# Ten extra products after the transposes of q for tile 1, in the opening of a fused attention, MLP and soft-MoE kernel

## The chip, the cores and the metric

The kernel runs on one core of a Trainium2 chip. The metric is device microseconds of one execution; a kernel's figure is the median of its runs. The engines are named as in the profile: PE is TensorE (PEld its weight loads), DVE is VectorE, ACT is ScalarE, POOL is GpSimd, and SP issues the DMAs. [...]

## The reference

Three stages follow one another, all in float32.

```
k_p, v_p = means of k and v over 8 neighbouring positions      # 576 -> 72 positions
attn = softmax(q @ k_p.T / 8);  x = attn @ v_p                 # 8 batches, 8 heads, head size 64
x = x.transpose(0, 2, 1, 3).reshape(4608, 512)
x = relu(x @ w_in)**2 @ w_out                                  # 512 -> 2048 -> 512
logits = x @ phi                                               # 32 slots
slots = softmax(logits over tokens).T @ x                      # 32 x 512
slots = relu(slots @ w1[e]) @ w2[e]                            # 8 experts, 4 slots each
out = softmax(logits over slots) @ slots
```

## The kernel before

The 4608 tokens are cut into 36 tiles of 128. A tile goes through attention first, then through the first layer of the MLP (`l1_half`), four quarters of 512 columns each. In the trace the first layer is L453: xh is the rounded high part of the attention's output x of a tile, xl the rest, and each quarter takes twelve products (four chunks of 128 rows; each is xh with the high part of w, xh with the low part of w, and xl with the high part of w).

The steps of attention of a tile t, with their lines:

- `att_qT`: four transposes of q on PE (L218), then one ACT copy into `acc` (L222). Every tile uses the same `acc`.
- `att_sc`: the scores, two halves of two products (L234) on PE; each half has its maxima taken on DVE (L241, `mx`).
- exponentials: tiles 0, 1 and 3 take eight small ACT instructions (L245, `es`); tile 2 adds the maxima on DVE (L250) and takes one ACT instruction (L259).
- `att_norm`: row sums, reciprocal and scaling on DVE (L266, L267, L268; L264 for tile 2).
- `att_aT`: eight transposes on PE (L299), two ACT copies (L300).
- `att_av`: sixteen products on PE (L311), then xh on ACT (L318) and xl on DVE (L319).

Before the first layer can run, w_in has to be converted, a chunk of 128 rows at a time: one ACT instruction (L342), four DVE instructions and one that may run on either (L344, L347, L351, L355, L356; all on DVE here), an ACT cast to the high part (L395) and a POOL subtraction for the low part (L396). The names w_243, w_485 and w_578 in the rows of the order are the first three quarters of w_in before the change (w_243, w_496 and w_589 behind it); l_... are the PSUM tiles of the first layer. es_121 is the buffer of tiles 0 and 2, es_122 that of tiles 1 and 3.

The function `opening` issues tiles 0 to 3 and the first two quarters of w_in by hand; from there slots of a table take over. `early` and `behind` set priorities and order, but the final order on each engine's queue is made by a scheduler when the program is built: each engine runs its own queue strictly in that order, and an instruction that waits holds all that stand behind it on its engine. The opening already holds two groups of products of the identity with itself, whose result nobody reads (named `warm`): eleven before the first data arrive (L957) and six behind the transposes of q of tile 0 (L684, the line of `behind`).

Of the kernel before, what the change touches and what calls it, by code (L numbers as in the profile page):

```python
# [8 lines left out]
F32 = mybir.dt.float32  # L9
# [8 lines left out]
def kernel(  # L18
# [12 lines left out]
    nc = tc.nc  # L31
# [4 lines left out]
    E, _, F = w1.shape  # L36
# [3 lines left out]
    P = 128  # L40
# [28 lines left out]
    ps1 = ctx.enter_context(tc.tile_pool(name="ps1", bufs=1, space=bass.MemoryType.PSUM))  # L69
# [7 lines left out]
    ident = const.tile([P, P], F32, tag="ident", name="ident")  # L77
# [136 lines left out]
    def att_qT(t):  # L214
        qt = q_t.pop(t)
        pq = ps("gT" if t in (0, 2, 4, 6, 8, 10, 12, 14, 16, 18, 20, 22, 24, 26, 28, 29, 30, 31, 33) else "att")
        for i in range(NPAIR):
            mark["q0"] = nc.tensor.transpose(  # L218
                pq[:, i * P:(i + 1) * P], qt[:, 2 * i:2 * i + 2].rearrange("p h d -> p (h d)"), ident
            )  # L220
        qT = acc.rearrange("p (a b) -> p a b", b=P)
        mark["qT", t] = nc.scalar.activation(out=qT.rearrange("p a b -> p (a b)"), in_=pq, func=AF.Copy)  # L222
        qT_t[t] = qT

    def att_sc(t):
        qT = qT_t.pop(t)
        es = es2[t % 2][:, :H * SP].rearrange("p (h s) -> p h s", s=SP)
        mx = a1.tile([P, H], F32, tag="mx", name="mx", bufs=8)
        for half in range(2):
            sc = ps("gT" if t in (0, 2, 4, 6, 8, 10, 12, 14, 16, 18, 20, 22, 24, 26, 28, 29, 30, 31, 33) else "att")  # L230
            for i in range(2):
                pi = 2 * half + i
                for off, n, b, s in parts(t):
                    mark["sc", t] = nc.tensor.matmul(  # L234
                        sc[off:off + n, i * 2 * SP:(i + 1) * 2 * SP],
                        qT[:, pi, off:off + n],
                        kb[b % 2][:, pi].rearrange("p a s -> p (a s)"),
                    )
            sv = sc[:, :HH * SP].rearrange("p (h s) -> p h s", s=SP)
            hs = slice(half * HH, (half + 1) * HH)  # L240
            mark["mx", t] = nc.vector.reduce_max(out=mx[:, hs], in_=sv, axis=AX.X, negate=True)  # L241
            if t in NXS:
                for h in range(HH):
                    e = half * HH + h
                    mark["es", t] = nc.scalar.activation(  # L245
                        out=es[:, e], in_=sv[:, h], func=AF.Exp, bias=mx[:, e:e + 1],
                        accum_out=rsum[:, t % 8, e, 0:1],
                    )
                continue
            nc.vector.tensor_tensor(  # L250
                out=es[:, hs], in0=sv, in1=mx[:, hs].unsqueeze(2).to_broadcast([P, HH, SP]), op=ALU.add
            )
        es_t[t] = es

    def att_exp(t):
        if t in NXS:
            return
        es = es_t[t]
        nc.scalar.activation(out=es, in_=es, func=AF.Exp)  # L259

    def att_norm(t):
        es = es_t[t]
        if t not in NXS:
            nc.vector.reduce_sum(out=rsum[:, t % 8, :, 0], in_=es, axis=AX.X)  # L264
        rs = a1.tile([P, H], F32, tag="rs", name="rs", bufs=4)
        nc.vector.reduce_sum(out=rs, in_=rsum[:, t % 8], axis=AX.X)  # L266
        nc.vector.reciprocal(out=rs, in_=rs)  # L267
        mark["norm", t] = nc.vector.tensor_tensor(out=es, in0=es, in1=rs.unsqueeze(2).to_broadcast([P, H, SP]), op=ALU.mult)  # L268
# [36 lines left out]
    def att_av(t):  # L305
        aT = aT_t.pop(t)
        px = ps("gT" if t in (0, 2, 4, 6, 8, 10, 12, 14, 16, 18, 20, 22, 24, 26, 28, 29, 30, 31, 33) else "att")
        for i in range(NPAIR):
            for off, n, b, s in parts(t):
                for e in range(2):  # L310
                    nc.tensor.matmul(  # L311
                        px[e * D:(e + 1) * D, i * P + off:i * P + off + n],
                        vp_t[b][:, 2 * i + e],
                        aT[:, 2 * i + e, off:off + n],
                    )
        xh = xp.tile([P, KD, P], F32R, tag="xh", name="xh")
        xl = xp.tile([P, KD, P], F32R, tag="xl", name="xl")
        nc.scalar.copy(out=xh.rearrange("p a b -> p (a b)"), in_=px)  # L318
        nc.vector.tensor_tensor(  # L319
            out=xl.rearrange("p a b -> p (a b)"),  # L320
            in0=px,
            in1=xh.rearrange("p a b -> p (a b)").bitcast(F32),
            op=ALU.subtract,
        )
        x_t[t] = (xh, xl)
# [36 lines left out]
    st_t, mark, n_st = {}, {}, [0]  # L362
# [24 lines left out]
    def conv_steps(j, kk):  # L387
        if kk == 0:
            wq.append(wp.tile([P, 2, KD, QF], F32R, tag="w", name=f"w{j}"))
        w = wq[j]  # L390
        steps = f32_steps(st_t["in", j][:, kk], eng=eng[AE[4 * j + kk]])
        for _ in range(3):
            c = next(steps)
            yield
        nc.scalar.copy(out=w[:, 0, kk], in_=c)  # L395
        nc.gpsimd.tensor_tensor(out=w[:, 1, kk], in0=c, in1=w[:, 0, kk].bitcast(F32), op=ALU.subtract)  # L396
        yield
# [282 lines left out]
    def behind(names, fn, *a):  # L680
        with ExitStack() as es:
            for n in names:
                es.enter_context(tc.issue_after(mark[n].ins))
            fn(*a)  # L684
# [5 lines left out]
    def new_big(shape, name, dtype=F32):  # L690
        pool, tag = ring[n_big[0] % len(ring)]
        n_big[0] += 1
        if pool == 1:
            return None, [late[1].tile([P] + shape[2:], dtype, tag=tag, name=name) for _ in range(4)]
        t = (late[pool] if pool in (0, 2) else pool).tile(shape, dtype, tag=tag, name=name)
        return t, [t[:, i] for i in range(4)]
# [73 lines left out]
    def early(fn, *a):  # L770
        with tc.high_priority():
            fn(*a)
# [175 lines left out]
    def opening():  # L948
        conv = {(j, kk): conv_steps(j, kk) for j in range(PC) for kk in range(KD)}

        def go(j, kk, n=4):
            for _ in range(n):
                next(conv[j, kk])

        warm = ps1.tile([P, P], F32, tag="pl", name="warm")
        for _ in range(11):
            nc.tensor.matmul(warm, ident, ident)  # L957
        early(kb_from, 0, pk0)
        go(0, 0, 2)
        early(att_qT, 0)  # L960
        warm = ps1.tile([P, P], F32, tag="pl", name="warm")
        for _ in range(6):
            behind(["q0"], nc.tensor.matmul, warm, ident, ident)
        go(0, 0, 1)
        behind([("qT", 0), "kbA"], go, 0, 0, 1)
        early(att_sc, 0)
        go(0, 1, 1)
        behind(["kbV"], go, 0, 1, 2)
        behind([("es", 0)], go, 0, 1, 1)
        early(att_norm, 0)  # L970
        for i in range(0, NPAIR, 2):
            behind([("sc", 0), ("es", 0)], pool_v, 0, i, kvp)
            behind([("mx", 0) if i == 0 else ("norm", 0)], pool_v_dve, 0, i + 1, kvp)
        go(0, 2, 1)
        behind([("mx", 0)], go, 0, 2, 2)
        behind([("es", 0)], go, 0, 2, 1)
        early(att_aT, 0)
        early(att_av, 0)
        go(0, 3, 3)
        behind([("aT", 0)], go, 0, 3, 1)  # L980
        for half in range(2):
            l1_half(0, 0, half)
        behind(["pv"], att_qT, 1)
        behind([("aT", 0)], att_sc, 1)
        att_norm(1)
        behind([("l1", 0, 0)], att_aT, 1)
        att_av(1)
        for t in (2, 3):
            att_qT(t)
            for kk in range(2):  # L990
                if t == 3:
                    go(1, kk)
            att_sc(t)
            att_exp(t)
            att_norm(t)
            att_aT(t)
            for kk in range(2, 4):
                if t == 3:
                    go(1, kk)
            att_av(t)  # L1000

    opening()
    nc.sync.dma_start(out=phi_sb, in_=phi.rearrange("(k p) s -> p k s", p=P))
    at(5, load_q, 4)
# [77 lines left out]
    cT_rest, _ = new_big([P, NT // 4 - NG, 4, P], "cT", F32R)  # L1082
# [94 lines left out]
```

## Time and profile before

| what | us |
|---|---|
| median of three runs | 774.43 (772.29 to 775.55) |
| the profiled execution | 766.02 |
| its span | 764.2 |

The profiled execution is the one whose trace is read here; its span leaves 1.82 us of its time outside. It is 8.41 us under the median of the runs. In the span PE is busy 95% of the time, DVE 70%, ACT 51%, POOL 17%. The page's line of granted clocks has a 6 for one slice of 40, the second one (19.1 to 38.2 us); in all others but the last it shows 9.

A timeline row reads: start, duration, engine, line, operation, tile written and tile read, shape, count, and in brackets the idle time before and what ended it. The records of a float32 product come in twos. Neighbouring records overlap by some tens of ns, so the step from one start to the next is the better measure of what an instruction costs in a full queue.

### The profile page before, as it was taken

What the parts mean: (1) busy time and instruction counts of PE and PEld (TensorE: products, weight loads), DVE (VectorE), ACT (ScalarE), POOL (GpSimd) and SP (SyncE); (2) the same over time, 40 slices, a digit from 0 to 9 for tenths busy, and PEclk for the clock granted to TensorE, in tenths of its full rate; (3) what the DMA queues carried; (4) which work ended last, traced back from release to release, by engine and by line L of the source; (5) the groups of instructions that cost most, each with busy time, mean ns of one, the idle gap of its engine ahead of it and who ended that gap; (6) DMA issues with size and microseconds to landing.
All of it is one profiled execution on the core that took longest, in us unless ns stands there. A gap on an engine that the chain in (4) does not pass through costs nothing.

```text
span 764.2 us, 14453 instructions
## 1 busy us (share of the span) xinstructions
PE 723.5 (95%) x5260; PEld 511.4 (67%) x5260; DVE 532.0 (70%) x1049; ACT 392.1 (51%) x1135; POOL 132.1 (17%) x151
## 2 busy tenths in 40 slices
PE   8789999989899999999999999999999999998992
PEld 7557788777677776676666666766666676663462
DVE  4996766596936689789979787878787746324153
ACT  3685677455547464545656562737575454341142
POOL 2231300052714400050342221320000000000000
PEclk9699999999999999999999999999999999999997
DMA  8956754858655996696997788878686436979998
GB/s 276 310 181 204 232 134 135 247 146 250 166 166 151 281 250 183 185 275 177 256 285 224 194 243 241 227 216 240 177 271 199 116 96 233 415 250 352 372 313 294
DMA packets 224135, 175.10 MB, mean 229 GB/s; under 512 B 75072, under 2 KB 186688, under 8 KB 224064
## 3 DMA queue, kind: packets, MB, share of 16 engines
q1 hardware_dynamic: 224064, 174.17, 75.2%
q8 instruction: 42, 0.69, 0.4%
q14 instruction: 29, 0.24, 0.1%
HBM read 126.94 MB, written 47.19 MB: 228 GB/s over the span
## 4 chain that ended last, share of the span: by engine, by line
PE 71%; DVE 12%; DMA 7%; ACT 6%; issue 2%; SPq 0%; POOL 0%; ACTq 0%; DVEq 0%
PE l L453 44%; PE misc L633 3%; PE pl L541 3%; PE misc L1098 2%; PE gT L311 2%; ACT es L245 2%; PE att L311 2%; PE l L1066 2%; PE gT L234 2%; PE att L234 2%; PE att L541 2%; DMA kv<-in_v_dram 1%; ACT aT L284 1%; DMA st<-in_moe_w_in_dram 1%; DMA out_dram<-o 1%
## 5 line engine op out<-in xcount | busy, mean ns | idle before, releaser
L453 PE MATMUL l<-w,xh 128*128 128x512 f32 x1152 | 383.4, 412 | 10.1 <-DVE g L473 5.0
L453 PEld LDWEIGHTS l<-w,xh 128*128 128x128 f32 x1152 | 209.8, 190 | 77.1 <-issue 17.1
L453 PE MATMUL l<-w,xl 128*128 128x512 f32 x576 | 231.7, 403 | 0.0
L466 ACT ACTIVATE r<-l 128x512 f32<-128x512 f32 x144 | 86.6, 604 | 163.6 <-PE l L453 151.1
L453 PEld LDWEIGHTS l<-w,xl 128*128 128x128 f32 x576 | 109.3, 190 | 28.7 <-issue 3.9
L157 POOL TENSOR_TENSOR kv<-kv 72x512 f32<-72x512 f32 x40 | 54.0, 1356 | 211.6 <-DMA kv<-in_v_dram 112.8
L284 ACT COPY aT<-turned 32x256 f32<-32x256 f32 (+1 forms) x168 | 67.8, 404 | 21.2 <-DVE turned L293 19.2
L473 DVE TENSOR_TENSOR g<-l,r 128x512 f32<-128x512 f32 x57 | 39.0, 683 | 28.0 <-ACT r L466 21.8
L245 ACT ACTIVATE es<-att,mx 128x72 f32<-128x72 f32 x120 | 36.9, 334 | 25.3 <-DVE mx L241 25.0
L516 DVE STREAM_TRANSPOSE turned<-turned 128x1024 f32<-128x1024 f32 x39 | 47.6, 1230 | 2.5 <-DMA turned<-g_dram 1.9
L245 ACT ACTIVATE es<-gT,mx 128x72 f32<-128x72 f32 x120 | 36.8, 331 | 16.0 <-DVE mx L241 15.9
L286 DVE COPY aT<-turned 32x256 f32<-32x256 f32 (+1 forms) x120 | 38.4, 320 | 1.6
L475 ACT ACTIVATE g<-r 128x512 f32<-128x512 f32 x54 | 34.5, 640 | 0.8
L396 POOL TENSOR_TENSOR w<-tmp,w 128x512 fp32r<-128x512 f32 x16 | 22.8, 1430 | 66.6 <-ACT w L395 66.6
L158 POOL TENSOR_TENSOR kv<-kv 72x256 f32<-72x256 f32 x40 | 33.1, 833 | 0.8
L473 DVE TENSOR_TENSOR tmp<-l,r 128x512 f32<-128x512 f32 x33 | 22.5, 682 | 15.4 <-ACT r L466 12.1
L268 DVE TENSOR_TENSOR es<-es,rs 128x576 f32<-128x576 f32 x36 | 32.3, 902 | 0.7
L344 DVE TENSOR_SCALAR tmp<-tmp 128x512 uint32<-128x512 uint32 x32 | 16.3, 511 | 23.3 <-ACT tmp L342 23.3
L516 DVE STREAM_TRANSPOSE tmp<-tmp 128x1024 f32<-128x1024 f32 x25 | 30.3, 1223 | 2.9 <-DMA tmp<-g_dram 2.9
L342 ACT ACTIVATE tmp<-st 128x512 f32<-128x512 f32 x32 | 21.7, 680 | 14.5 <-DMA st<-in_moe_w_in_dram 10.3
L245 ACT ACTIVATION_READ_ACCUMULATOR es<-att,mx 128x1 f32 x120 | 26.3, 219 | 0.0
L245 ACT ACTIVATION_READ_ACCUMULATOR es<-gT,mx 128x1 f32 x120 | 26.0, 217 | 0.0
(200 smaller groups left out, 1064.1 us busy)
## 6 DMA issues: line engine op xcount, KB each, us to landing
g_dram<-g SPq DMA_DIRECT2D x95, 256.0 KB
turned<-g_dram SPq DMA_DIRECT2D x39, 512.0 KB
w<-in_moe_w_dram SPq DMA_DIRECT2D x32, 512.0 KB
tmp<-g_dram SPq DMA_DIRECT2D x25, 512.0 KB
w<-in_moe_w_dram SPq DMA_DIRECT2D x6, 2048.0 KB
g_back<-g_dram SPq DMA_DIRECT2D x40, 256.0 KB
kv<-in_k_dram SPq DMA_DIRECT2D x32, 288.0 KB
kv<-in_v_dram SPq DMA_DIRECT2D x32, 288.0 KB
```

What stands on the lines that cost most here:

```text
L157: eng.tensor_tensor(out=x[:, :, 0:4], in0=x[:, :, 0:4], in1=x[:, :, 4:8], op=ALU.add)
L158: eng.tensor_tensor(out=x[:, :, 0:2], in0=x[:, :, 0:2], in1=x[:, :, 2:4], op=ALU.add)
L245: mark["es", t] = nc.scalar.activation(out=es[:, e], in_=sv[:, h], func=AF.Exp, bias=mx[:, e:e + 1], accum_out=rsum[:, t % 8, e, 0:1],)
L268: mark["norm", t] = nc.vector.tensor_tensor(out=es, in0=es, in1=rs.unsqueeze(2).to_broadcast([P, H, SP]), op=ALU.mult)
L284: nc.scalar.copy(out=dst, in_=src)
L286: eng[e].tensor_copy(dst, src)
L453: mm = mark["l1", t, j] = nc.tensor.matmul(hp_t[t, j], steps[i][0], steps[i][1], start=(i == 0), stop=(i == 2 * n - 1))
L466: nc.scalar.activation(out=r, in_=hp, func=AF.Relu, scale=1.0 / (R * R if sq == "V" else R))
L473: mark["sq"] = nc.vector.tensor_tensor(out=dst, in0=pre, in1=src, op=ALU.mult)
L475: nc.scalar.activation(out=dst, in_=src, func=AF.Square)
L516: nc.vector.transpose(out=gc.rearrange("p (n i) -> p n i", i=32), in_=gc.rearrange("p (n f) -> p n f", f=32))
L541: mark["logits"] = nc.tensor.matmul(pl[32 * c:32 * c + 32], a_sb[:, c, 32 * j:32 * j + 32], gT[:, c], start=(alone or j == 0), stop=(alone ...
```

## The change

Behind the four transposes of q of tile 1, and ahead of that tile's scores, ten products of the identity with itself are issued into a fresh PSUM tile of the tag `pl`. Nothing reads their result.

```diff
         behind(["pv"], att_qT, 1)
+        warm = ps1.tile([P, P], F32, tag="pl", name="warm")
+        for _ in range(10):
+            mark["warm"] = behind(["q0"], nc.tensor.matmul, warm, ident, ident)
         behind([("aT", 0)], att_sc, 1)
```

The queue of PE at that place, around the transposes of tile 1 (L218) and its scores (L234 into att); rows with + are new:

```order
 L182 MATMUL l_306<-kv_148,ident 72x128 x8
 L218 MATMUL att<-ident,qt 128x128 x4
+L684 MATMUL warm<-ident 128x128 x10
 L234 MATMUL att<-kb_119,acc 128x144 x4
 L299 MATMUL gT<-ident,es_121 72x128 x8
```

The ten products stand between the two steps of tile 1; all that stood ahead of them is as it was. Behind them the scheduler laid out the rest of the opening anew. The queues of PE, ACT and DVE differ from there to the attention of tiles 2 and 3, and from then on all queues hold the same work in the same order; POOL's and SP's do so throughout.

On ACT, the stretch around xh of tile 1 (L318), the copy of q of tile 3 (L222) and the casts of the second quarter of w_in (L395), before:

```order
L342 ACTIVATE tmp<-st 128x512
L259 ACTIVATE es_121<-es_121 128x576
L318 CAST xh<-att 128x512
L222 ACTIVATE acc<-att 128x512
L395 CAST w_485<-tmp 128x512 x2
L245 ACTIVATE es_122,rsum<-att,mx 128x72 x8
```

and now:

```order
L259 ACTIVATE es_121<-es_121 128x576
L300 COPY aT<-att 72x512 x2
L342 ACTIVATE tmp<-st 128x512
L395 CAST w_496<-tmp 128x512
L318 CAST xh<-att 128x512
L222 ACTIVATE acc<-att 128x512
L395 CAST w_496<-tmp 128x512
L245 ACTIVATE es_122,rsum<-att,mx 128x72 x8
```

The third cast of that quarter has moved from behind xh and the copy of q to ahead of them; it waits for a DVE instruction (L356).

On DVE, from the conversion of the second chunk of that quarter (the first L356 here) on, before:

```order
L356 SCALAR_TENSOR_TENSOR tmp<-tmp 128x512
L250 TENSOR_TENSOR es_121<-gT,mx 128x288
L351 SCALAR_TENSOR_TENSOR tmp<-st,tmp 128x512
L241 TENSOR_REDUCE mx<-gT 128x4
L344 TENSOR_SCALAR tmp<-tmp 128x512
L347 TENSOR_SCALAR tmp<-tmp 128x512
L355 TENSOR_TENSOR tmp<-tmp 128x512
L250 TENSOR_TENSOR es_121<-gT,mx 128x288
L351 SCALAR_TENSOR_TENSOR tmp<-st,tmp 128x512
L356 SCALAR_TENSOR_TENSOR tmp<-tmp 128x512
```

and now:

```order
L356 SCALAR_TENSOR_TENSOR tmp<-tmp 128x512
L268 TENSOR_TENSOR es_122<-es_122,rs 128x576
L250 TENSOR_TENSOR es_121<-gT,mx 128x288
L351 SCALAR_TENSOR_TENSOR tmp<-st,tmp 128x512
L344 TENSOR_SCALAR tmp<-tmp 128x512
L347 TENSOR_SCALAR tmp<-tmp 128x512
L355 TENSOR_TENSOR tmp<-tmp 128x512
L264 TENSOR_REDUCE rsum<-es_121 128x8
L351 SCALAR_TENSOR_TENSOR tmp<-st,tmp 128x512
L356 SCALAR_TENSOR_TENSOR tmp<-tmp 128x512
```

The scaling of tile 1 (L268 on es_122) has moved behind the first L356 (it stood four places ahead of it), the row sums of tile 2 (L264) have moved ahead of the second L356, and one half of tile 2's maxima and of L250 have moved ahead of this stretch.

## Rows read from the trace of the kernel before

**Rows 1.** Busy time by stretch; per engine us (count), then PEclk, DMA share, GB/s.

```profile
26.00:30.00 4.00, 4.00 (x27) 3.12 (x26) 4.00 (x8) 3.00 (x12) 0.90 (x1) 0.50 0.91 227
...
40.00:50.00 10.00, 8.22 (x48) 5.49 (x45) 10.00 (x19) 6.57 (x24) 2.98 (x3) 1.00 0.73 246
...
60.00:70.00 10.00, 10.00 (x64) 7.67 (x63) 8.33 (x11) 5.50 (x10) 1.74 (x1) 1.00 0.46 137
```

**Rows 2.** Timeline, opening, three engines: start, duration, engine, line.

```profile
2.04 4.63 PE L957 MATMUL warm<-ident 128*128 128x128 f32 x22 [2.04 <-POOL ident masks.py:199]
...
12.82 1.60 PE L684 MATMUL warm<-ident 128*128 128x128 f32 x12
...
19.73 0.66 PE L218 MATMUL att<-ident,qt 128*128 128x128 f32 x4 [0.47 <-DMA qt<-in_q_dram]
...
22.19 0.62 ACT L222 ACTIVATE acc<-att 128x512 f32<-128x512 f32 x1
...
22.86 2.06 PE L234 MATMUL att<-kb,acc 128*128 128x144 f32 x8 [2.48 <-ACT acc L222]
...
27.34 0.80 DVE L241 TENSOR_REDUCE mx<-att 128x4 f32<-128x288 f32 x2
```

**Rows 3.** Busy time in short stretches around changes of the granted clock.

```profile
23.10:23.20 0.10, 0.10 (x2) 0.10 (x2) 0.10 (x1) 0.00 (x0) 0.10 (x1) 0.68 1.22 440
...
36.70:36.80 0.10, 0.10 (x2) 0.10 (x1) 0.10 (x1) 0.00 (x0) 0.10 (x1) 0.56 1.07 369
...
156.20:156.40 0.20, 0.20 (x3) 0.14 (x2) 0.20 (x2) 0.00 (x0) 0.20 (x1) 0.64 1.11 384
...
159.60:159.80 0.20, 0.20 (x2) 0.12 (x2) 0.20 (x1) 0.20 (x3) 0.20 (x2) 0.83 0.97 346
```

**Rows 4.** Timeline of PE ahead of the second fall of the clock.

```profile
155.01 0.74 PE L453 MATMUL l<-w,xh 128*128 128x512 f32 x2 [1.60 <-DVE g L473]
```

**Rows 5.** Timeline, DVE alone, a stretch with nothing between its instructions.

```profile
41.40 0.44 DVE L250 TENSOR_TENSOR es<-gT,mx 128x288 f32<-128x288 f32 x1
41.76 0.68 DVE L351 SCALAR_TENSOR_TENSOR tmp<-st,tmp 128x512 f32<-128x512 uint32 x1
42.36 0.68 DVE L356 SCALAR_TENSOR_TENSOR tmp<-tmp 128x512 uint32<-128x512 uint32 x1
42.96 0.41 DVE L344 TENSOR_SCALAR tmp<-tmp 128x512 uint32<-128x512 uint32 x1
43.30 0.68 DVE L355 TENSOR_TENSOR tmp<-tmp 128x512 f32<-128x512 f32 x1
43.90 0.74 DVE L264 TENSOR_REDUCE rsum<-es 128x8 f32<-128x576 f32 x1
44.56 1.11 DVE L347 TENSOR_SCALAR tmp<-tmp 128x512 uint32<-128x512 uint32 x1
```

**Rows 6.** Timeline: one POOL run, and a DVE instruction beside the next.

```profile
44.12 1.27 POOL L396 TENSOR_TENSOR w<-tmp,w 128x512 fp32r<-128x512 f32 x1 [3.87 <-ACT w L395]
...
48.31 1.30 DVE L355 TENSOR_TENSOR tmp<-tmp 128x512 f32<-128x512 f32 x1
```

**Rows 7.** Timeline, from xh of tile 1 to the last attention of the opening.

```profile
42.46 0.58 ACT L318 CAST xh<-att 128x512 fp32r<-128x512 f32 x1
...
47.84 0.45 DVE L241 TENSOR_REDUCE mx<-att 128x4 f32<-128x288 f32 x1
...
49.72 0.24 ACT L245 ACTIVATION_READ_ACCUMULATOR es<-att,mx 128x1 f32 x1
...
50.80 0.15 DVE L266 TENSOR_REDUCE rs<-rsum 128x8 f32<-128x16 f32 x1
...
51.23 0.76 DVE L268 TENSOR_TENSOR es<-es,rs 128x576 f32<-128x576 f32 x1
...
52.13 1.04 PE L299 MATMUL att<-ident,es 128*72 128x128 f32 x8 [0.74 <-DVE es L268]
...
55.64 1.14 PE L311 MATMUL att<-aT,vp 72*64 72x128 f32 x16 [0.58 <-ACT aT L300]
```

## The prediction

> **What bounds the kernel now.** I read the page first, then busy time by stretch, then the timeline of the opening. After the opening TensorE is the bound: from 60 to 70 us it is busy for 10.00 of 10 us [rows 1], and this goes on with few gaps to the end. So the change can act in two ways only: it moves the moment at which that dense stretch begins, or it adds work to it. It adds none there; the ten products stand in the opening.
>
> In the opening TensorE is not the bound. From 40 to 50 us VectorE is busy for 10.00 of 10 us and TensorE for 8.22; from 26 to 30 us VectorE again has no gap while TensorE runs at a granted clock of 0.50, and is busy for all of that time only because it takes twice as long [rows 1]. The rows of VectorE there follow each other without a hole: each start is the one before plus 0.34 to 0.66 us [rows 5]. These are the conversions of w_in, the maxima, and the scaling of attention.
>
> The idle time that the change fills is plain: the transposes of q of tile 1 start at 19.73 and end at 20.39, and the scores of that tile start at 22.86, after 2.48 us in which TensorE waited for the copy on ScalarE, which ends at 22.81 [rows 2]. [...] A second fall, at 156.3 until 159.7, came 1.3 us after a gap of 1.60 us [rows 3, 4].
>
> The point where VectorE hands over to TensorE is the end of tile 3's attention. The last maxima of that tile start at 47.84, the last exponential ends at 49.96, two small instructions follow on VectorE from 50.80, the scaling starts at 51.23, the transposes at 52.13, and the last attention products, behind which TensorE never waits for long, at 55.64 [rows 7]. I therefore ask how far the changed order moves that 55.64.
>
> **The ten products.** Six such products took 1.60 us at full clock, 0.267 each; ten take 2.67 us [rows 2]. Begun at 20.39 they end at 23.06, and the scores start 0.2 us late. Were the clock at half, the eleven products at the start of the program give 0.42 each (4.63 over 11) [rows 2]; the ten would then end at 24.6 and the scores start 1.7 us late. Either is covered: the two maxima that read these scores stand on VectorE behind a reduction, a conversion step and more, at 27.34 before [rows 2] and later now; at half clock the scores take 2.06 us [rows 2] and are done at 26.7. Cost 0; without that cover 0.2 to 1.7 us.
>
> **The clock.** With the gap filled I expect the granted clock to stay at 1.00 past 23.2. At most this gives back half of 13.6 us, 6.8 us of TensorE time. I put its worth on the path at 0, since VectorE, with no hole in those stretches [rows 1, 5], does not get its own work done sooner when TensorE is faster.
>
> **What the new order moves.** This is the larger part. Steps from one start to the next are taken from [rows 5]: 0.60 for L351, L355 and L356, 0.34 for L344 (and L347, which has the same shape), 0.36 for L250 (and L241, which is as long), 0.66 for L264 (and L268, over the same 576 columns).
>
> First, ScalarE now has the cast of the third chunk of the second quarter ahead of xh of tile 1 and the copy of q of tile 3. It waits for the second L356 of the rows of the order. Compared with before, only the row sums L264 are newly ahead of that L356 (L268 stands ahead of it in both orders), so it ends at 42.96 + 0.66 = 43.6. The cast takes about as long as the cast L318, 0.58 [rows 7], and xh starts at 44.2 instead of 42.46 [rows 7], 1.7 us later. Behind xh wait the copy of q and then the scores of tile 3. Their maxima are taken far later on VectorE (next step), which covers this. It costs TensorE something else: it has nothing to do between the transposes of tile 3's q, which before ended just ahead of 42.46 where xh starts, and the cast's end at 44.2, a gap of some 1.8 us.
>
> Second, the last maxima of tile 3. Ahead of them stand three instructions that came right behind them before: a reciprocal (a tenth), a conversion step (0.60) and the scaling of tile 2 (0.66), 1.4 us. A third POOL run also falls ahead of them. Beside POOL's subtractions instructions of VectorE are stretched: L347 at 44.56 took 1.11 us where L344, of the same shape, took 0.41, and L355 at 48.31 took 1.30 where it took 0.68 at 43.30 [rows 5, 6]; so one run costs about 0.65. Together 2.0 us: the last maxima end at 48.2 + 2.0 = 50.2. The exponentials end 1.76 us behind them (49.96 less 48.20) [rows 7], at 52.0, and the scaling starts 0.43 later (51.23 less 50.80), at 52.4 instead of 51.23: 1.2 us late. In the old order the scaling stood behind other work of VectorE when the exponentials were done; now VectorE waits for them.
>
> How POOL's runs fall is the unknown. Of each of the three runs VectorE may lose nothing (if what it does there is a reduction or reads PSUM) or the whole 1.27 us of a run [rows 6]. With nothing lost the scaling starts at about 50.3, 0.9 us early; with all lost at about 54.1, 2.9 us late. I take 0.65 a run, as the rows have it.
>
> [...] The stretched rows [rows 5, 6] show a block of about half a run. [...]
>
> Third, the tail. From the scaling to the last attention products it took 55.64 less 51.23, 4.41 us [rows 7]; there ScalarE was late, with squares, copies and xh of tile 2 ahead of the copies of tile 3. In the new order that work is mostly done while VectorE waits. TensorE then does: the start of the transposes 0.90 behind the scaling (52.13 less 51.23), the transposes 1.04 [rows 7], half of tile 2's attention products 0.57 (half of 1.14) [rows 7], the four transposes of tile 4's q 0.66 [rows 2]. That is 3.17 us, 1.24 less.
>
> The sum so far: +1.2 - 1.24 = 0.0, with bounds of -0.9 - 1.24 = -2.1 and +2.9 - 1.24 = +1.7.
>
> Fourth, the gap of 1.8 us on TensorE ahead of the cast is as long as the 1.60 us that was followed by the second fall. If the clock falls there and is back after 3.4 us as in that case [rows 3, 4], TensorE does 1.7 us less work. In 40 to 50 us it had 1.78 us without work [rows 1], so most of it is covered; between 0 and 1.7 us I take 0.4.
>
> So the profiled execution of 766.02 us becomes 766.4. Against the median of the runs, which lies 8.41 us higher, the same +0.4 gives **774.8 us**: no change that can be told. A difference under 0.5% (3.9 us) is about what a measurement of this kernel can't tell from none.
>
> **The rivals.**
>
> *The dummies don't hold the clock.* At full clock the scores take half of 2.06 us and are done at 24.1; then TensorE waits for VectorE to scale tile 0. If the clock falls a few us later than before, it is at half until about the same 36.8 [rows 3]. The order is the new one all the same. The half of the scores that VectorE wants first then costs it at most the 1.03 us by which they take longer; I take 0.6. For it: work that takes half the time leaves gaps about as long as before. Against it: the one long gap, 2.48 us, is filled. Time: 774.8 + 0.6 = 775.4.
>
> [...]
>
> *The clock falls late (slower).* The gap ahead of the cast, about 42.4 to 44.2, is followed by a fall as long as the first, 13.6 us, just where the products of the second quarter and tile 3 stand. Half of that, 6.8 us, is lost, less the 1.78 us of idle time of 40 to 50 us [rows 1]: +5.0 over the sum of 0.0, or 779.4 us. It decides when the gap grows beyond 1.6 us and the clock isn't back by 50 us. For it: the gap is new, and the first fall lasted that long [rows 3]. Against it: the second fall, amid dense products, lasted 3.4 us only.
>
> *TensorE is the bound after all (faster).* Then the 6.8 us at half clock come back, less 0.2 for the products: 774.43 - 6.6 = 767.8. For it: 13.6 us at half clock in a kernel that TensorE bounds. Against it: VectorE has no hole from 26 to 30 and from 40 to 50 us [rows 1].
>
> **How the numbers follow.** Forecast 0.53; the clock not held 0.17; the whole lock 0.08; the late fall 0.13; TensorE the bound 0.09. The first three lie within 0.5% of 774.43 (770.6 to 778.3), 0.78; a part of 0.01 on each side for what the later waits make of a shift, which leaves same 0.76, faster 0.10, slower 0.14. The forecast's own range is 772.3 to 776.5 (-2.1 to +2.1 around the median, the upper end 1.7 and 0.4). For 8 in 10 it reaches toward the faster and the slower case: 770.0 to 779.0.
>
> **What would show it.** Right: granted clock 1.00 from 23 to 27 us; ten products from 20.4 to about 23.1; no hole on VectorE until the last maxima of tile 3, then a wait of about 1 us for the exponentials; xh of tile 1 at about 44.2, a TensorE gap of about 1.8 us before it; the last attention products within 2 us of 55.6. Wrong: VectorE idle between 23 and 45 us, so that TensorE sets the pace there; those last products before 53 or after 58 us; or a shift made in the opening that is gone or doubled by 200 us.

## The result, and the profile after

The changed kernel is slower: a median of 778.95 us over 6 runs (778.17 to 780.06) against 772.69 over 6 runs of the kernel before beside it (769.76 to 775.55). The ratio is 1.008, with a 95% interval of 1.0053 to 1.0108: 0.8%, some 6 us. The median lies 0.05 us inside the upper end of the predicted range, which was drawn that wide for the slower rival; that is luck. The forecast, no change that can be told, is wrong. Here and below a ratio is that of the runs within 1.5% of the fastest of their kernel, and not the quotient of the two medians, which are of all runs. The profiled execution took 779.36 us, its span is 777.6.

Busy time by stretch of the kernel after, the same columns as in [rows 1]:

```profile
10.50:20.50 10.00, 10.00 (x118) 9.86 (x115) 4.73 (x10) 3.45 (x6) 1.29 (x1) 0.50 1.02 293
24.80:27.00 2.20, 2.20 (x22) 2.20 (x21) 2.20 (x5) 1.27 (x3) 1.33 (x1) 1.00 1.01 275
27.00:28.20 1.20, 1.16 (x10) 0.94 (x8) 1.20 (x4) 0.69 (x1) 0.01 (x1) 1.00 0.87 153
34.70:40.90 6.20, 5.46 (x14) 4.07 (x15) 5.62 (x11) 4.27 (x20) 1.82 (x1) 0.50 0.99 330
45.00:55.00 10.00, 7.96 (x46) 5.92 (x45) 10.00 (x17) 4.46 (x8) 4.31 (x3) 0.83 0.51 165
51.80:54.60 2.80, 2.80 (x12) 2.40 (x10) 2.80 (x4) 0.62 (x1) 1.52 (x2) 0.50 0.99 379
65.00:71.50 6.50, 6.50 (x42) 5.25 (x38) 2.54 (x4) 1.25 (x3) 1.26 (x1) 0.50 0.17 46
72.00:80.00 8.00, 8.00 (x56) 6.05 (x55) 5.63 (x11) 4.98 (x9) 1.39 (x1) 1.00 0.42 115
```

From 45 to 55 us VectorE is busy for 10.00 of 10 us, as from 40 to 50 before; from 27.0 to 28.2 the scores run at full clock; and the half-speed stretch (granted clock 0.50) that came at 23.2 and lasted until 36.8 before, 13.6 us [rows 3], now comes at 34.2 and lasts 6.8. The first row is not the change's doing. The clock stood at 0.50 from about 10 to 20 us, ahead of all that was changed, and it did so in 9 of the 14 profiles of this study, the kernel before among them. It puts the transposes of q of tile 1 at 24.34 instead of 19.73; in the nine profiles they start at 22.77 to 25.98, in the other five at 19.73 to 20.55. From here on I therefore count from the start of those transposes, and call it S.

TensorE in the changed kernel (start, duration, line), to be laid beside [rows 2, 7]:

```profile
24.34 0.60 PE L218 MATMUL att<-ident,qt 128*128 128x128 f32 x4
24.78 2.40 PE L684 MATMUL warm<-ident 128*128 128x128 f32 x20
27.01 1.15 PE L234 MATMUL att<-kb,acc 128*128 128x144 f32 x8
...
50.50 1.49 PE L453 MATMUL l<-w,xh 128*128 128x512 f32 x3 [1.99 <-ACT w L395]
...
59.72 0.66 PE L311 MATMUL gT<-aT,vp 72*64 72x128 f32 x8 [1.00 <-ACT aT L300]
...
63.73 1.14 PE L311 MATMUL att<-aT,vp 72*64 72x128 f32 x16 [1.19 <-ACT aT L300]
```

The products fill their gap at full clock, and the scores behind them take 1.15 us where they took 2.06. The last attention products come at S + 39.39 instead of S + 35.91 (63.73 less 24.34; 55.64 less 19.73). So 3.5 us are lost between these two marks. VectorE shows where (start, duration, line, and idle time ahead with its releaser):

```profile
32.89 1.12 DVE L347 TENSOR_SCALAR tmp<-tmp 128x512 uint32<-128x512 uint32 x1
...
38.03 0.46 DVE L241 TENSOR_REDUCE mx<-gT 128x4 f32<-128x288 f32 x1 [0.58 <-PE gT L234]
...
39.08 1.69 DVE L356 SCALAR_TENSOR_TENSOR tmp<-tmp 128x512 uint32<-128x512 uint32 x1
...
42.10 1.07 DVE L344 TENSOR_SCALAR tmp<-tmp 128x512 uint32<-128x512 uint32 x1
...
45.06 1.59 DVE L351 SCALAR_TENSOR_TENSOR tmp<-st,tmp 128x512 f32<-128x512 uint32 x1
...
51.18 1.65 DVE L356 SCALAR_TENSOR_TENSOR tmp<-tmp 128x512 uint32<-128x512 uint32 x1
...
53.95 1.83 DVE L268 TENSOR_TENSOR es<-es,rs 128x576 f32<-128x576 f32 x1
...
56.67 0.45 DVE L241 TENSOR_REDUCE mx<-att 128x4 f32<-128x288 f32 x1
...
58.74 0.17 DVE L266 TENSOR_REDUCE rs<-rsum 128x8 f32<-128x16 f32 x1 [1.03 <-ACT es L245]
...
59.18 0.76 DVE L268 TENSOR_TENSOR es<-es,rs 128x576 f32<-128x576 f32 x1
```

Six instructions are stretched ahead of the last maxima (56.67): by 0.71, 1.01, 0.66, 0.91, 0.97 and 1.08 us against the undisturbed ones of their lines (0.41 for L344 and L347, 0.68 for L351 and L356, 0.75 for L268), 5.34 in all. Two waits are new, 0.58 for TensorE's scores of tile 2, which ran at half clock, and 1.03 for the exponentials of tile 3 (0.66 and 1.1 from the time at which a full queue would have started the instruction). In the old order VectorE had no hole here and lost 3.45 us in five stretched instructions, four of them ahead of the last maxima.

The dense stretch begins with the ReLU (L466) at 61.77 before, S + 42.04, and at 73.05 now, S + 48.71. Of these 6.7 us, 3.5 are the opening's; the other 3.2 fit the half clock of 65.0 to 71.5. There TensorE is busy throughout, and its products of the first layer (L453) follow each other at 0.43 us where they do so at 0.23 to 0.24 from 72 to 80, at a clock of 1.00; by that some 3.0 of the 6.5 us are lost, an estimate. From there the shift stays between 6.1 and 7.7 us (with S taken out; one ReLU shows 4.8) until 360 us.

### The profile page after: what moved, and what is told of

It is laid out like the page before. It is cut to its first block, busy times and chain, and to the rows that moved or that the text cites. A ratio compares the mean times of both kernels' runs of the same rounds, so it can differ in the third digit from the quotient of the medians.

```text
span 777.6 us, 14493 instructions
## 1 busy us (share of the span) xinstructions
PE 732.1 (94%) x5280; PEld 519.8 (67%) x5280; DVE 533.9 (69%) x1049; ACT 391.8 (50%) x1135; POOL 135.7 (17%) x151
## 4 chain that ended last, share of the span: by engine, by line
PE 68%; DVE 15%; DMA 7%; ACT 5%; issue 2%; SPq 1%; POOL 0%; DVEq 0%; ACTq 0%
PE l L453 41%; PE misc L633 3%; PE pl L541 3%; PE misc L1101 2%; PE gT L234 2%; PE gT L311 2%; DVE es L268 2%; PE att L311 2%; PE l L1069 2%; PE att L164 2%; DMA turned<-g_dram 2%; ACT es L245 2%; DMA kv<-in_v_dram 2%; PE att L234 1%; PE att L541 1%
## 5 line engine op out<-in xcount | busy, mean ns | idle before, releaser
L453 PE MATMUL l<-w,xh 128*128 128x512 f32 x1152 | 385.1, 414 | 13.9 <-DVE g L473 4.3
L453 PEld LDWEIGHTS l<-w,xh 128*128 128x128 f32 x1152 | 210.6, 191 | 81.2 <-issue 16.2
L453 PE MATMUL l<-w,xl 128*128 128x512 f32 x576 | 232.0, 403 | 0.0
L466 ACT ACTIVATE r<-l 128x512 f32<-128x512 f32 x144 | 86.5, 603 | 167.1 <-PE l L453 155.8
L453 PEld LDWEIGHTS l<-w,xl 128*128 128x128 f32 x576 | 110.0, 191 | 28.7 <-issue 3.9
L245 ACT ACTIVATE es<-gT,mx 128x72 f32<-128x72 f32 x120 | 36.8, 332 | 15.8 <-DVE mx L241 15.8
L396 POOL TENSOR_TENSOR w<-tmp,w 128x512 fp32r<-128x512 f32 x16 | 26.4, 1651 | 74.1 <-ACT w L395 68.1
L344 DVE TENSOR_SCALAR tmp<-tmp 128x512 uint32<-128x512 uint32 x32 | 15.1, 471 | 27.8 <-ACT tmp L342 27.8
L268 DVE TENSOR_TENSOR es<-es,rs 128x576 f32<-128x576 f32 x36 | 33.7, 940 | 0.7
```

The costliest lines, as they stand in the source:

```text
L245: mark["es", t] = nc.scalar.activation(out=es[:, e], in_=sv[:, h], func=AF.Exp, bias=mx[:, e:e + 1], accum_out=rsum[:, t % 8, e, 0:1],)
L453: mm = mark["l1", t, j] = nc.tensor.matmul(hp_t[t, j], steps[i][0], steps[i][1], start=(i == 0), stop=(i == 2 * n - 1))
L466: nc.scalar.activation(out=r, in_=hp, func=AF.Relu, scale=1.0 / (R * R if sq == "V" else R))
```

## The experiments

The diff does two things at once: it adds ten products, and it makes the scheduler lay out PE, ACT and DVE anew. To take these apart I wrote the queues' orders out: each instruction of the opening got an order-only edge to the next one of a list, so that a kernel can have either order with or without the products. In the traces the queues of VectorE and ScalarE then follow the order that each kernel was given.

```diff
+ORDER = {"PE": (104, [...]), "DVE": (30, [...]), "Activation": (18, [...])}
+def pin(nc, tc, dummies=(), at=None):
...
         tile_pooled_attention__moe__soft_moe_kernel(tc, *args)
+        pin(nc, tc, DUMMIES, 136)
```

**The new order without the products** (the kernel before, with the lists of the changed one):

> The order of the queues that the change brings, without the ten products. If the new order is the cause (theory A): slower than before by 5 to 7 us, the last attention products of tile 3 (L311 on att) some 3 to 4 us later than in the old order, measured from the transposes of q of tile 1. If the cause is the half-speed time that the products push to a later place (theory B): within 1.5 us of before, and the granted clock falls at about 23 us, ahead of the stretch that TensorE bounds, as before. If it takes both: 2 to 4 us slower.

Measured: 776.59 us against 773.31, ratio 1.0037 (1.0007 to 1.0067). By the time this is the third case, 2 to 4 us; by the profile (below) it is theory A.

**The old order with the products** (the changed kernel, with the lists of the one before):

> The ten products at their place, every other instruction of every queue in the order of the kernel before. Theory A (order): within 1.5 us of before, or up to 2 us faster, since the clock is held over the gap at no cost. Theory B (half-speed time moved): slower by 4 to 7 us, with a fall of the granted clock between 40 and 75 us, where TensorE sets the pace.

Measured: 770.84 us, ratio 0.9983 (0.9948 to 1.0017).

**The changed kernel and the kernel before, on the same chip:**

> The changed kernel once more, on the chip of the others: 5 to 7 us slower than before by either theory. Its profile shows whether the fall of the clock at 10 us, ahead of the new products, is there each time (it cost 3.9 us in the first profile and can't come from the products behind it); if it is chance, this profile need not have it, and the difference of the spans is then 6 to 9 us and not 13.

> The kernel before once more: ratio 1.000. Its profile shows whether a fall of the clock at 10 us comes without the change too: its first profile, at 766.0 us, lay 4 to 9 us under its timed runs, as it would if most of those have that fall. Theory A and B say nothing on it; if it shows here, the first pair of profiles overstates the change by 3.9 us.

Measured: 779.98 us, ratio 1.0079 (1.0045 to 1.0112), and 772.39 us, ratio 0.9988 (0.9965 to 1.0011). From S to the last attention products it took 35.08 us in the kernel before, 34.71 in the old order with the products, 39.56 in the new order alone, 38.87 in the changed kernel. The order costs 4.2 to 4.5 us there; the products take 0.4 to 0.7 off in these four profiles. What the medians leave open is the products in the new order, 3.4 us; a later pair bears on that.

**Which queue?** First VectorE's old order within the new one of the others, then ScalarE's.

```diff
-    "DVE": (30, [... L189, L355, L344, L241, L347, L241, L356 ...])
+    "DVE": (30, [... L189, L241, L241, L355, L344, L347, L344, L356 ...])
```

> No products. TensorE and ScalarE in the order of the changed kernel, VectorE's queue in the order of the kernel before; the other queues are the same in both. The new order of all three cost 2.9 us of the median (776.59 against 773.31 for the kernel before on that chip) and 3.5 to 4.5 us of the opening: from the transposes of q of tile 1 to the last attention products of tile 3 it took 39.56 us, against 35.08 to 35.91 with the old order. Theory V, the cost lies in VectorE's queue (it meets five runs of GpSimd instead of four in the stretch, and takes an instruction of the next quarter ahead of the maxima that the chain needs): the stretch takes 35 to 36.5 us, and the time is that of the kernel before within 1 us, about 773. Theory S, the cost lies in ScalarE's queue (xh of tile 0 and the copy of q of tile 2 are taken among the exponentials of tile 1, and the third cast ahead of xh of tile 1): the stretch stays at 38.5 to 40 us, and the time 2 to 4 us above the kernel before, about 776. If both carry a part, 37 to 38 us.

Measured: 777.92 us, ratio 1.0056 (1.0027 to 1.0085); the stretch took 41.22 us.

```diff
-    "Activation": (18, [... L245, L318, L245 x3, L222, L245 x4 ...])
+    "Activation": (18, [... L245 x8, L318, L222 ...])
```

> No products. TensorE and VectorE in the order of the changed kernel, ScalarE's queue in the order of the kernel before. The mirror image of the run with VectorE's old order. Theory V: the stretch from the transposes of q of tile 1 to the last attention products of tile 3 stays at 38.5 to 40 us, the time 2 to 4 us above the kernel before, about 776. Theory S: 35 to 36.5 us, about 773. A third possibility is that VectorE's new order without ScalarE's waits still longer, since its first instructions of tile 2 need what ScalarE now does later: over 40 us, 777 or more.

Measured: 782.88 us, ratio 1.0126 (1.0076 to 1.0175); the stretch took 43.75 us. Both V and S fail: neither queue's old order alone brings the 35 to 36 us back. Against the 39.56 us of the new order alone they are 1.7 and 4.2 us longer, but a second profile of that kernel (below) took 41.07, so only ScalarE's lies clear of it. There the scaling of tile 3 starts as late as with VectorE's old order (S + 36.38 and S + 36.37); the rest is lost behind it, where TensorE waited 2.71 us for ScalarE's copies of tile 2 and the clock was at half from 59.2 to 72.9. In both kernels VectorE waited for ScalarE or TensorE for 4.1 us up to that scaling. With VectorE's old order its stretched instructions cost 3.91 us only, but it waited at these places:

```profile
33.50 0.17 DVE L266 TENSOR_REDUCE rs<-rsum 128x8 f32<-128x16 f32 x1 [1.45 <-ACT es L245]
...
43.79 0.43 DVE L344 TENSOR_SCALAR tmp<-tmp 128x512 uint32<-128x512 uint32 x1 [1.62 <-ACT tmp L342]
...
48.86 0.43 DVE L344 TENSOR_SCALAR tmp<-tmp 128x512 uint32<-128x512 uint32 x1 [1.06 <-ACT tmp L342]
```

So I turned to single exchanges that the new order allows.

**One exchange in the new order.**

```diff
-L189, L355, L344, L241, L347, L241
+L189, L241, L241, L355, L344, L347
```

> No products. The new order of all three queues with one exchange on VectorE: behind the first sum over v (L189) the two maxima of tile 1 (L241) come ahead of the first two instructions of the next conversion (L355, L344), as in the kernel before. In the new order GpSimd's subtraction beside that sum took 3.82 us, in the old one 1.27; the only thing that differs there is what VectorE runs next: SBUF to SBUF in the new order, from PSUM in the old. Theory V1, that neighbour makes the long run and the long run costs the chain: the subtraction takes 1.3 us again, the maxima of tile 1 come 1 to 2 us earlier, the stretch from the transposes of q of tile 1 to the last attention products takes 37.5 to 38.5 us instead of 39.56, and the time falls by 1 to 2 us against the whole new order (to 774.5 to 775.5 where the kernel before takes 773.3). Rival, the long run lies beside waits and the order further on sets the end: the subtraction may shrink, but the stretch stays at 39 to 40 us and the time at about 776.5.

Measured: 774.69 us, ratio 1.0044 (1.0005 to 1.0083); the stretch took 38.89 us, VectorE lost 4.62 us in stretched instructions instead of 5.34. GpSimd's run beside L189, of this kernel:

```profile
26.33 1.27 POOL L396 TENSOR_TENSOR w<-tmp,w 128x512 fp32r<-128x512 f32 x1 [1.88 <-ACT w L395]
```

and of the new order alone:

```profile
29.42 3.82 POOL L396 TENSOR_TENSOR w<-tmp,w 128x512 fp32r<-128x512 f32 x1 [2.88 <-ACT w L395]
```

Theory V1 holds for the run. Its price in the profile is 0.7 us of the 4, the size of the one stretched instruction that is gone (L347, 0.71), and less than the 1 to 2 us that were expected. In the time no gain shows: the ratio is 1.0044 where the whole new order has 1.0037.

**A second exchange on top**, ahead of the last maxima:

```diff
-L351, L268, L241, L355, L241, L356, L266
+L351, L241, L355, L241, L268, L356, L266
```

> No products. The new order of all three queues with two exchanges on VectorE: the two maxima of tile 1 ahead of the next conversion, as in the run with the first exchange alone (38.89 us from the transposes of q of tile 1 to the last attention products, 0.7 less than the new order, GpSimd's run 1.27 us instead of 3.82), and the two maxima of tile 3 ahead of the scaling of tile 2. In the new order VectorE waited 1.03 us for the exponentials of tile 3, which it did not in the old one: there a conversion and the scaling of tile 2 stood between the last maxima and the sum that needs the exponentials, in the new one a single instruction. Theory W, that wait is made by the order of these few instructions: it goes, and the stretch takes 37.7 to 38.0 us; the time falls by another 1 us, to 1 to 2 us above the kernel before. Rival, the exponentials themselves are late because ScalarE is: the wait comes back elsewhere, and the stretch stays at 38.7 to 39.0 us.

Measured: 774.71 us against 771.85, ratio 1.0051 (1.0021 to 1.0081). The stretch took 36.79 us. VectorE at its end:

```profile
52.69 0.45 DVE L241 TENSOR_REDUCE mx<-att 128x4 f32<-128x288 f32 x1
53.05 1.41 DVE L355 TENSOR_TENSOR tmp<-tmp 128x512 f32<-128x512 f32 x1
...
54.38 0.45 DVE L241 TENSOR_REDUCE mx<-att 128x4 f32<-128x288 f32 x1
54.75 0.74 DVE L268 TENSOR_TENSOR es<-es,rs 128x576 f32<-128x576 f32 x1
...
55.41 0.68 DVE L356 SCALAR_TENSOR_TENSOR tmp<-tmp 128x512 uint32<-128x512 uint32 x1
...
56.22 0.17 DVE L266 TENSOR_REDUCE rs<-rsum 128x8 f32<-128x16 f32 x1
```

The wait for the exponentials is gone, and the stretch is 2.1 us shorter than with one exchange, twice what W gave: beside GpSimd's run now stands L355, stretched by 0.73, in place of the scaling with its 1.08, and the wait for the scores of tile 2 did not occur in this profile. Two exchanges of a few instructions thus give back 2.8 of the 4.2 to 4.5 us in the profile. The times don't show the second either: the median is 2.9 us above the kernel before beside it, where one exchange was 1.1 above in another set of runs, and the ratios are 1.0051 and 1.0044.

**More products.**

```diff
-        for _ in range(10):
+        for _ in range(20):
             behind(["q0"], lambda: DUMMIES.append(nc.tensor.matmul(warm, ident, ident).ins))
```

> The order of the kernel before on all queues, with twenty instead of ten products behind the transposes of q of tile 1. If the products cost nothing in the opening, because the scores of tile 1 that stand behind them are not what VectorE waits for, twenty cost nothing either: twenty end about 5 us after the transposes begin, the scores about 6.3 us after, and VectorE takes their maxima at about 7.6 us in the old order; the stretch to the last attention products stays at 34.7 to 36.0 us, the time at 770 to 773 us beside 773.3 for the kernel before. If they do cost (the scores of tile 1 are the bound, or the products take from others), ten more cost 1.5 to 2.7 us: the stretch 36.5 to 38.5 us, the time 773 to 776.

Measured: 775.76 us against 771.85, ratio 1.0061 (1.0027 to 1.0096). TensorE and the maxima behind them:

```profile
24.52 0.60 PE L218 MATMUL att<-ident,qt 128*128 128x128 f32 x4
24.96 4.63 PE L986 MATMUL warm<-ident 128*128 128x128 f32 x40
...
29.43 1.15 PE L234 MATMUL att<-kb,acc 128*128 128x144 f32 x8
31.32 0.81 DVE L241 TENSOR_REDUCE mx<-att 128x4 f32<-128x288 f32 x2
```

In the profile twenty cost nothing in the opening: the scores start 2.2 us later than with ten and still end 0.7 us ahead of their maxima, and the stretch took 35.08 us, as in the kernel before. The median is 3.9 us slower all the same. The profile (span 772.7) shows no place for it: the shift with S taken out is -0.8 us at the start of the dense stretch, as in the second profile of the kernel before. Where the runs lose it stays open.

**Filling an earlier wait too**, that for q of tile 0:

```diff
+        for _ in range(8):
+            FILL.append(nc.tensor.matmul(warm, ident, ident).ins)
...
+            if e == "PE" and n == 10:
+                seq.extend(FILL)
```

> The order of the kernel before on all queues, with the ten products behind the transposes of q of tile 1, and eight more products of the same kind in the wait for q of tile 0: behind the first eleven products of the pooling of k, ahead of the transposes of q of tile 0. In all the profiles but the first of the kernel before, that wait ended at 8.87 to 9.79 us and the granted clock stood at 0.50 from about 10 us to 19.6 to 22.7 us, which put the transposes of q of tile 1 at 23.7 to 26.0 us instead of 19.73. Theory C, the idle 1.2 to 2.3 us of that wait let the clock fall: with the eight products (about 1.7 to 2.2 us of work) it stays at 1.00 to 20 us or longer in the profile, the transposes of q of tile 1 start at 19.5 to 21 us, and the time is 3 to 4 us under that of the kernel before, 768 to 770 where that takes 773; it would be the fastest kernel here. Rival, the fall does not come from that wait: the clock falls at about 10 us all the same and the time is that of the old order with the ten products alone, 771 to 772, or up to 1 us longer for the products in the way.

Measured: 772.64 us, ratio 1.0013 (0.998 to 1.0046). The clock was at 1.00 from 8 to 20 us here, but so it was in the three other profiles of the same set, one of which waited 1.98 us for that q. So the profile doesn't bear out theory C, and there is no gain in the time. What makes the clock fall at 10 us stays open.

**The order alone and the changed kernel once more, side by side:**

> The new order without the products once more, beside the changed kernel, since by the medians of the first four runs the order cost 3.3 us and the products in that order another 3.4, while in the profiles the products took 0.4 to 0.7 us off the opening in either order. Theory A, the order is the whole cost: 776 to 779 us, within 1.5 us of the changed kernel beside it. Theory B, the products cost about 3 us in this order: 775.5 to 777, and the changed kernel 779 to 781.

> The changed kernel once more, beside the new order without the products. Theory A: 776 to 779 us, within 1.5 us of the new order alone. Theory B: 779 to 781 us, about 3 us above it. In its profile the stretch from the transposes of q of tile 1 to the last attention products is 38.5 to 39.5 us in either case.

Measured: 778.21 us, ratio 1.0117 (1.0072 to 1.0161), for the order alone, and 777.22, ratio 1.0076 (1.0041 to 1.011), for the changed kernel. The two lie 1.0 us apart, as theory A (the order is the whole cost) has it. Over both pairs the order alone is 3.3 and 6.4 us above the kernel before beside it, the changed kernel 6.3, 6.7 and 5.4, so the order carries most of the loss, and 1 or 2 us for the products in that order are neither shown nor excluded. Without the products the clock fell just ahead of the scores of tile 1 in this profile, so that these took 2.29 us, 1.15 at full clock, and the opening took 41.07 us, 2.0 more than with them beside it (39.06):

```profile
24.53 6.42 POOL L396 TENSOR_TENSOR w<-tmp,w 128x512 fp32r<-128x512 f32 x1 [5.69 <-ACT w L395]
...
25.16 2.29 PE L234 MATMUL att<-kb,acc 128*128 128x144 f32 x8 [1.79 <-ACT acc L222]
...
31.68 0.43 DVE L344 TENSOR_SCALAR tmp<-tmp 128x512 uint32<-128x512 uint32 x1 [1.85 <-ACT tmp L342]
```

GpSimd's run took 6.42 us and handed 1.85 us of it back to VectorE, through ScalarE's next conversion, which waited 5.87 us for the run.

## Why the prediction was wrong

The prediction's own sign of being wrong is there: with S's delay taken out the last attention products come at 59.12, behind 58. The account, from the ten profiles with a whole order (us; stretched and waits: VectorE, from L189 in front of the maxima of tile 1 to the scaling of tile 3, a wait counted from where a full queue would have started the instruction):

| profile | order, products | S to last attention products | stretched | waits | start of the dense stretch, S taken out, against before |
|---|---|---|---|---|---|
| before | old, 0 | 35.91 | 3.45 | 0 | 0 |
| before again | old, 0 | 35.08 | 3.17 | 0 | -0.8 |
| old order | old, 10 | 34.71 | 3.14 | 0 | -1.2 |
| old order, bridged | old, 10 | 35.64 | 3.16 | 0 | -0.3 |
| old order, twenty | old, 20 | 35.08 | 3.44 | 0 | -0.8 |
| new order alone | new, 0 | 39.56 | 5.34 | 1.8 | +3.7 |
| new order again | new, 0 | 41.07 | 5.61 | 4.0 | +6.8 |
| after | new, 10 | 39.39 | 5.34 | 1.8 | +6.7 |
| changed again | new, 10 | 38.87 | 5.37 | 1.8 | +3.0 |
| changed, third | new, 10 | 39.06 | 5.33 | 1.1 | +4.8 |

The last column follows the ReLU that stands at 61.77 before. Its mean is -0.6 us in the old order and +5.0 in the new one: 5.6 us, where the three comparisons of the changed kernel gave 6.1 on average. So by these profiles nearly all of the loss is made by 75 us.

*The ten products, cost 0:* right in the profiles. They ran as forecast (2.40 us for 2.67) and the scores behind them were not waited for, with twenty neither. The 0.42 us a product for half clock was too low: the eleven it is read from ran from 2.04 to 6.67 at a granted clock of 1.00, and the six behind q of tile 0, at 0.50 in the changed kernel, took 2.93 us (from 16.49), 0.49 each.

*The clock, worth 0:* right in the old order. With the products the scores ran at full clock, and the opening took 34.71 to 35.64 us where it took 35.08 and 35.91 without them, so the faster rival (TensorE is the bound) falls. The rival that the products don't hold the clock is right in part. They put the fall off: it came 7.0 to 13.0 us behind S in the six profiles with products, 1.4 to 6.7 in the eight without. But it came, at 34.2 in the changed kernel, and the scores of tile 2 then ran at half clock and cost VectorE 0.66 us, the size of that rival's 0.6.

*Xh of tile 1 and the gap ahead of it:* right in kind. Xh came 3.3 us late (50.35, S + 26.01, for S + 22.73) instead of 1.7: the products that it reads ended at 47.92, but the cast ahead of it on ScalarE's queue started at 49.83 only, after 2.42 us in which it waited for VectorE (L356). The gap was 1.99 for 1.8, and the clock fell behind it, from 51.8 to 54.6. VectorE shows no wait from 38.5 to 58.7, so this fall cost the chain nothing there.

*The last maxima of tile 3, +2.0: the step that failed.* They came at S + 32.33 instead of S + 28.11, 4.2 us late. The three instructions ahead of them, 1.4 us, stand as worked out. GpSimd's runs do not: "one run costs about 0.65", and one more run was counted. There were two more stretched instructions ahead of the maxima, and they lost 0.66 to 1.08 us each: 5.34 less 2.83, 2.5 us for the 0.65 of the sum. The bound "of each of the three runs" looked at the runs near the end and left out that the new order sends the runs of the whole stretch onto other instructions (redone from its own terms, both ends come out 0.2 us later, which changes nothing). The reading "a block of about half a run" was wrong too: each instruction lost what was left of the run when its turn came (last section), 0.75 to 0.87 us in the five meetings before, 0.78 to 1.21 in the six now, less about 0.13. That nothing is lost by a reduction or by what reads PSUM, the lower bound, the trace of before shows beside GpSimd's runs: the row sums L264 took 0.74 us (43.90) and the maxima L241 0.44 and 0.45 (35.70, 39.02), where that whole trace has 0.71 to 0.75 and 0.41 to 0.46 for these lines. That a whole run is lost at each of three meetings, the 1.7 us above the forecast to which the whole lock's chance of 0.08 belongs, no run shows: six meetings cost 0.66 to 1.08 us each. Their stretches are 1.9 us above the forecast, which is near the 1.7 by chance. The remaining 0.3 is a wait that the forecast had at none, 0.66 us for the scores of tile 2, less 0.35 by which VectorE was early at L189.

*The wait for the exponentials:* right, 1.03 us, and included in the sum. The scaling came 2.5 us behind the last maxima instead of 3.4.

*The tail, -1.24:* wrong. It took 4.55 us (59.18 to 63.73) instead of 4.41. The work that was to be done while VectorE waits was not: ScalarE's queue has the eight exponentials of tile 3 ahead of the copies of tile 2, and squares, a conversion and xh of tile 2 between those and the copies of tile 3. TensorE waited 1.00 us for the first copies and 1.19 for the second:

```profile
59.07 1.08 ACT L300 COPY aT<-gT 72x512 f32<-72x512 f32 x2
...
63.05 1.12 ACT L300 COPY aT<-att 72x512 f32<-72x512 f32 x2
```

Reading only where an instruction stands on its own queue, I had not asked what that queue holds ahead of it.

*The clock in the dense stretch, +0.4:* the price was wrong, and the place. Behind the waits of that tail the clock fell at about 65 us in three of the five profiles in the new order (after, new order again, changed third), at the cost of 3.2, 1.6 and 1.6 us, and in none of the five in the old one. That is 1.3 us on average. The slower rival had a fall of the clock amid dense products with a price of 5.0 us, behind another gap; its time, 779.4, comes near by luck, for the most part for another reason.

So the sum for the changed order should have been about +4 us to the last attention products and +1.3 behind them.

What stays open: what the runs lose with twenty products (ratio 1.0061 in the old order, between the two of the new order alone), why the exchanges shorten the profile and not the time, and the fall at 10 us. The runs of one kernel spread over up to 13 us, more than such an exchange gives. The clock is a likely part of that, not a shown one: besides the falls at 10 us and in the tail each profile has one to three more between 150 and 440 us, of 3.4 or 6.8 us and not all at the same places (3.4 us from 156.3 and from 200.6 in the first profile of the kernel before, from 167.3 in that of the changed one), and over the 86 runs of the kernel before beside these kernels the time goes down as the mean granted clock goes up (correlation -0.76). No version here was shown to be faster than the kernel before.

## What to carry to other kernels

An instruction whose own cost can't be seen can cost 0.8% by where the scheduler puts everything behind it: look at the new order first, and pin the old one if only the instruction is wanted. When an order changes, go through all meetings of GpSimd and VectorE in the whole stretch, price each by what is left of GpSimd's run (0.75 to 1.21 us in the eleven meetings above, of which all but about 0.13 was lost), and go through what each queue holds ahead of the next link of the chain; one queue's old order within the new plan of the others gave nothing back here. Filling a gap on an engine that was not the bound gave no gain that could be told, though it put the fall of that engine's clock off, from 1.4 to 6.7 us behind S to 7.0 to 13.0.

## What the runs showed of the hardware

Where a VectorE instruction of the conversion or the scaling was stretched beside GpSimd's subtraction (L396), it ended a fixed time behind the subtraction, a little less than it takes alone. In the 93 such meetings from 20 to 66 us, over all fourteen profiles, it ended 0.28 to 0.30 us behind the run (L344 and L347, 0.41 alone), 0.54 to 0.56 (L351, L355 and L356, 0.68 alone) or 0.61 to 0.62 (L268, 0.75 alone). Where the subtraction started while such an instruction was at work, it was longer itself in some places: the changed kernel's at 50.52, inside an L355 that began at 50.14 and with an L347 right behind it, took 1.76 us where the shortest of that kernel took 1.26. Two runs of the changed kernel, to be laid beside L344 at 42.10 (until 43.17) and L268 at 53.95 (until 55.78) above:

```profile
41.53 1.35 POOL L396 TENSOR_TENSOR w<-tmp,w 128x512 fp32r<-128x512 f32 x1 [1.31 <-ACT w L395]
...
53.56 1.60 POOL L396 TENSOR_TENSOR w<-tmp,w 128x512 fp32r<-128x512 f32 x1 [1.28 <-ACT w L395]
```

and one of the kernel before, beside L355 at 48.31 (until 49.61) of [rows 6]:

```profile
47.60 1.46 POOL L396 TENSOR_TENSOR w<-tmp,w 128x512 fp32r<-128x512 f32 x1 [2.21 <-ACT w L395]
```

GpSimd's subtraction (L396) that started some 0.1 us into the sum over v (L189, from SBUF, 1.92 us) took 1.27 or 1.28 us in all eight profiles in which VectorE's next instruction was the maxima, which read PSUM, and 3.82 to 3.86 in all five in which it was L355, from SBUF to SBUF; in the fourteenth the run had started earlier, and took 6.42. The sum itself took 1.89 to 1.95 us in all of them. The single exchange of these instructions turned 3.82 into 1.27. So in these profiles the length of GpSimd's run went with what VectorE had next, and not only with what it did at the moment; by what mechanism was not shown. In the changed kernel the run of 3.83 us ended at 33.73, 1.21 us behind the start of VectorE's next maxima (32.52), which read PSUM; the short runs took 1.27 or 1.28 us in all.

The clock did not fall by the length of a wait alone. TensorE's wait for q of tile 0 was 0.42, 0.97, 1.15 and 1.98 us in profiles without a fall at 10 us, and 1.15 to 2.38 us in profiles with one.
